# A linear-attention and MLP kernel: one layer-norm output turned by a DMA transpose instead of by TensorE, with the engines' orders around it rewritten

## The chip, the core and the metric

The kernel runs on one core of a Trainium2 chip. A core has five engines with a queue of their own each: TensorE (PE, matrix products, with a separate row PEld for the loading of its weights), VectorE (DVE), ScalarE (ACT), GpSimd (POOL) and SyncE (SP), which here only issues DMA transfers. The metric is the device time of one execution in microseconds, median over several runs.

## What is computed

Two layers, each a linear attention block and an MLP, on x of 2048 rows and 512 columns in bfloat16, 32 heads of 16, an inner width of 1792:

```python
phi = lambda t: jnp.where(t > 0, t + 1, jnp.exp(t)) + 1e-6
pq, pk = phi(q), phi(k)
kv = jnp.einsum("bhsd,bhse->bhde", pk, v)
z = jnp.einsum("bhsd->bhd", pk)
num = jnp.einsum("bhqd,bhde->bhqe", pq, kv)
den = jnp.einsum("bhqd,bhd->bhq", pq, z)[..., None] + 1e-6
...
x = x + _A_ref(_layernorm(x, axis=-1), A_wqkv, A_wo)
x = x + _B_ref(_layernorm(x, axis=-1), B_w1, B_b1, B_w2, B_b2)
x = x + _A_ref(_layernorm(x, axis=-1), A_wqkv, A_wo)
x = x + _B_ref(_layernorm(x, axis=-1), B_w1, B_b1, B_w2, B_b2)
```

`_B_ref` is gelu(y @ w1 + b1) @ w2 + b2.

## The kernel before

The 2048 rows are 16 tiles of 128 rows (0 to 15), four to a chunk (chunks 0 to 3). x stays in SBUF in float32 (`xsb`), the weights too. The kernel is a graph of operations, each with a name, an engine and the names of what it reads and writes. The order on each engine is written out by hand in the table `ORDER`, one list of names for each of PE, ACT, DVE, POOL and SP; a second table, `WAY`, says for some operations which of two ways or engines they take. The class `Scheduler` replays the lists in a model of the engines to hand out buffers and PSUM banks (the earliest free one that a class of tiles allows); `assign_waits` then sets the semaphore waits that the dependencies need. Each engine runs its list strictly in order, so an instruction that waits holds everything behind it on that engine.

How to read a name: the digit behind the letters is the layer (0 or 1), then comes the tile, or the chunk and a part of it. The stage in question is in layer two (layer digit 1), from the end of its attention to its MLP:

- `K1_t`, `Q1_c_k` are the key and query products, `expk`, `reluk`, `mink`, `phik` (and `expq` to `phiq`) the steps of phi on ACT and DVE or POOL. `G1_c_dc` are the products of a chunk's keys with its inputs, four of them; `ga1_...` and `gt1_...` add them up on DVE. `za`, `zhi`, `zlo`, `ZH1`, `Z1_3`, `zs`, `dz1`, `zb1`, `ZR1` make z and what is derived from it. `KV1`, `kvm1`, `M1` and `cpm1` fold kv and wo into one matrix.
- The denominators: chunk 0 by `D1_0_k` on PE and `ln`, `rec` on ACT; chunks 1 to 3 by `pz` (product with z), `red` (sum over a head), `den` (add 1e-6) and `rec` (reciprocal) on DVE or POOL. `pr` divides; for chunks 1 to 3 `TP1_c_k` then turns the tile by DMA.
- `WO1_t` (L1110) is the attention's output product of a tile, four matmuls into a bank of class `w` (banks 3 to 5, at most two tiles at a time in the scheduler's count). `RA1_t` (L1115) adds it to x on DVE and so frees the bank.
- The layer norm of the MLP's input: `statsB1_t` (L743) and `aggrB1_t` (L745) on DVE, `vepsB1_t` (L748) and `powB1_t` (L758, the inverse root) on POOL, then `normB1_t` on DVE (L783), or on ACT (L778) with `nmrB1_t` (L775) on POOL ahead of it.
- The normalised tile is turned into chunk buffer `yT`. There are two ways: `TB1_t`, one DMA transpose issued by SP (L793); or `PTB1_t` (L806), four TensorE transposes of 128x128 into a PSUM bank, and `tcB1_t` (L816), a copy from there on ACT. Before the change tile 0 goes the second way and tiles 1 to 15 the first.
- `W11_c_ft_h` (L1142) is one of 14 sums of the first MLP product. Chunk 0 is split in halves: h = 0 reads tiles 0 and 1 (256 columns), h = 1 tiles 2 and 3. The other chunks take all four tiles at once. `gelu1_...` (L1148) on ACT empties the bank (class `h`, banks 0 to 3).
- `W21_t_0` and `W21_t_7` (L1181) are the two halves, seven matmuls each, of the second MLP product of a tile; `RB1_t` (L1187, L1191) adds x, `OD` stores the result. `b21_t` (L1127) adds b2 to x on DVE or POOL.

ACT holds one table of functions at a time; gelu needs another than exp and ln, and each change is a table load.

The choice between the two ways of turning is made here:

```python
if eng(f"TB{L}_{st}") == "pe":
    transpose_pe(y, ykey, yT, k, f"yB{L}_{st}", prio, f"B{L}_{st}", True)
else:
    transpose(y, ykey, yT, k, f"yB{L}_{st}", prio, f"B{L}_{st}")
```

Of the kernel before, what the change touches and what calls it, by code (L numbers as in the profile page):

```python
# [1377 lines left out]
```

## Time and profile before

| what | value |
|---|---|
| median of 3 runs (lowest to highest) | 325.28 us (325.04 to 326.11) |
| the profiled execution, its own time | 324.83 us |
| its span, first to last instruction | 323.1 us |
| granted TensorE clock | 1.000 |
| busy: PE, DVE, ACT, POOL | 319.6, 215.8, 194.8, 136.4 us |
| DMA transposes of normalised tiles (L793), of attention tiles (L1078) | 58, 20 |

The profile is of one execution. Times in its rows are microseconds from the first instruction of the span. A row of the timeline has start, length, engine, line, operation, tile written <- tiles read, shapes and count; neighbours of one kind are merged, "x4" being four instructions. The bracket behind a row is idle time of the engine before it and who ended it. The ends of matmuls are modelled and overlap the next start, so TensorE is read from start to start. An ACT or DVE instruction also overlaps its neighbour by about 0.1 us at the ends. Only the engines' own work counts as busy, not the issuing of DMAs or waits.

### The profile page before, as it was taken

What the parts mean: (1) busy time and instruction counts of PE and PEld (TensorE: products, weight loads), DVE (VectorE), ACT (ScalarE), POOL (GpSimd) and SP (SyncE); (2) the same over time, 40 slices, a digit from 0 to 9 for tenths busy, and PEclk for the clock granted to TensorE, in tenths of its full rate; (3) what the DMA queues carried; (4) which work ended last, traced back from release to release, by engine and by line L of the source; (5) the groups of instructions that cost most, each with busy time, mean ns of one, the idle gap of its engine ahead of it and who ended that gap; (6) DMA issues with size and microseconds to landing.
All of it is one profiled execution on the core that took longest, in us unless ns stands there. A gap on an engine that the chain in (4) does not pass through costs nothing.

```text
span 323.1 us, 4792 instructions
## 1 busy us (share of the span) xinstructions
PE 319.6 (99%) x1725; PEld 159.0 (49%) x1725; DVE 215.8 (67%) x506; ACT 194.8 (60%) x334; POOL 136.4 (42%) x224
## 2 busy tenths in 40 slices
PE   8999999999999999999999999999999999999996
PEld 4444445675444444444444444458644444444443
DVE  5998769999985660314659999999898664000232
ACT  6999798873136139488974657879913734576000
POOL 4564376638703359000367645874902934000000
DMA  7534576213320105310003200121242242000004
GB/s 244 178 68 83 148 234 224 49 35 64 67 49 16 35 16 98 67 32 3 0 0 68 49 16 2 25 57 36 50 80 53 49 67 65 16 0 2 32 24 156
DMA packets 48116, 20.65 MB, mean 64 GB/s; under 512 B 43164, under 2 KB 46620, under 8 KB 48092
## 3 DMA queue, kind: packets, MB, share of 16 engines
q1 hardware_dynamic: 46620, 15.32, 20.7%
q0 software_dynamic: 1056, 4.72, 4.6%
q10 hardware_dynamic: 416, 0.30, 0.3%
q8 instruction: 14, 0.23, 0.3%
q14 instruction: 10, 0.08, 0.1%
...
## 4 chain that ended last, share of the span: by engine, by line
PE 92%; DVE 6%; POOL 1%; ACT 0%; issue 0%
PE ps L1142 30%; PE ps L1181 29%; PE ps L861 8%; PE ps L1110 7%; PE ps L962 4%; PE ps L879 3%; PE ps L892 3%; PE ps L994 2%; PE ps L699 1%; PE ps L1168 1%; DVE gtb L1007 1%; DVE rd L1065 1%; PE ps L943 1%; DVE xsb L1115 1%; DVE gacc L1004 1%; PE ps L1086 1%
## 5 line engine op out<-in xcount | busy, mean ns | idle before, releaser
L1148 ACT ACTIVATE gT<-ps,b1c 128x512 bf16<-128x512 f32 (+1 forms) x140 | 77.3, 601 | 64.3 <-PE ps L1142 63.4
L1142 PE MATMUL ps<-t,w 128*128 128x512 bf16 (+1 forms) x560 | 101.2, 336 | 0.0
L1181 PE MATMUL ps<-w,gT 128*128 128x512 bf16 x434 | 98.4, 379 | 0.0
L1142 PEld LDWEIGHTS ps<-t,w 128*128 128x128 bf16 x560 | 54.6, 98 | 43.7 <-ACT t L816 0.3
L1181 PEld LDWEIGHTS ps<-w,gT 128*128 128x128 bf16 x434 | 42.4, 98 | 50.0
L758 POOL TENSOR_TENSOR rstd<-veps,neghalf 128x1 f32<-128x1 f32 x64 | 39.8, 633 | 5.2 <-DVE veps L756 3.0
L1191 DVE TENSOR_TENSOR pkb<-ps,xsb 128x512 bf16<-128x512 f32 x15 | 10.2, 685 | 41.4 <-PE ps L1181 41.4
L831 ACT ACTIVATE eb<-ps 128x512 bf16<-128x512 f32 x56 | 32.4, 598 | 9.0 <-PE ps L879 3.7
L743 DVE BATCH_NORM_STATS2 stats<-xsb 128x6 f32<-128x512 f32 x48 | 32.1, 677 | 0.3
L861 PE MATMUL ps<-wqkv,t 128*128 128x512 bf16 x128 | 31.8, 379 | 0.1
L1110 PE MATMUL ps<-gtb,t 128*128 128x512 bf16 x128 | 31.2, 379 | 0.1
L842 ACT ACTIVATE rb<-ps 128x512 bf16<-128x512 f32 x38 | 22.5, 601 | 10.5 <-PE ps L861 7.2
L748 POOL TENSOR_SCALAR veps<-mv 128x1 f32<-128x1 f32 x32 | 9.1, 283 | 42.8 <-DVE mv L745 40.8
L756 POOL TENSOR_SCALAR veps<-mv 128x1 f32<-128x1 f32 x28 | 7.5, 270 | 44.4 <-DVE mv L745 42.9
L778 ACT ACTIVATE yb<-xsb,nmr,rstd 128x512 bf16<-128x512 f32 x21 | 16.7, 811 | 11.4 <-POOL nmr L775 11.4
L783 DVE TENSOR_SCALAR yb<-xsb,mv,rstd 128x512 bf16<-128x512 f32 x27 | 14.9, 559 | 11.9 <-POOL rstd L758 11.8
L1187 DVE TENSOR_TENSOR xsb<-ps,xsb 128x512 f32<-128x512 f32 x16 | 10.9, 682 | 16.7 <-PE ps L1181 16.7
L879 PE MATMUL ps<-wqkv,t 128*128 128x512 bf16 x80 | 20.4, 379 | 0.0
L861 PEld LDWEIGHTS ps<-wqkv,t 128*128 128x128 bf16 x128 | 12.2, 97 | 15.2 <-ACT t L816 0.6
L1110 PEld LDWEIGHTS ps<-gtb,t 128*128 128x128 bf16 x128 | 12.4, 98 | 14.7 <-ACT gtb L975 0.3
L844 DVE TENSOR_SCALAR eb<-eb 128x512 bf16<-128x512 bf16 x46 | 14.0, 313 | 7.1 <-ACT eb L831 6.9
L1127 POOL TENSOR_TENSOR xsb<-xsb,b2b 128x512 f32<-128x512 f32 x14 | 17.1, 1219 | 1.0 <-DVE yb L783 0.7
...
## 6 DMA issues: line engine op xcount, KB each, us to landing
...
t<-yb SPq DMA_TRANSPOSE x58, 2.5
...
t<-t SPq DMA_TRANSPOSE x20, 2.5
```

The lines of the kernel that those rows point to most:

```text
L743: G.op("dve", lambda e: e.bn_stats(stats[:, s.slot, :], src()), 602, reads=src_keys, writes=[k + "s"], tiles=[s, *src_tiles], prio=prio, n ...
L758: G.op("pool", lambda e: e.tensor_tensor(rstd[:, s.slot:s.slot + 1], veps[:, s.slot:s.slot + 1], neghalf[:], op=ALU.pow), 530, reads=[k + ...
L778: G.op("act", lambda e: e.activation(yb[:, y.slot, :], src(), ACT.Identity, bias=nmr[:, s.slot:s.slot + 1], scale=rstd[:, s.slot:s.slot + 1]),
L831: G.op("act", lambda e: e.activation(eb[:, et.slot, :], bank(bt), ACT.Exp, scale=factor()), 569 if by else 483, reads=[src_key, *more], wr ...
L842: G.op("act", lambda e: e.activation(rb[:, rt.slot, :], bank(bt), ACT.Relu, scale=factor()), 569 if by else 478, reads=[src_key, *more], w ...
L861: ins = e.matmul(bank(b), lhsT=yTa(yT)[:, dt, k * P:(k + 1) * P], rhs=wqkv[:, dt, D:2 * D], start=(dt == 0), stop=(dt == DT - 1))
L879: ins = e.matmul(bank(b), lhsT=yTa(yT)[:, dt, k * P:(k + 1) * P], rhs=wqkv[:, dt, 0:D], start=(dt == 0), stop=(dt == DT - 1))
L1110: ins = e.matmul(bank(wb), lhsT=yTa(pq)[:, kt, k * P:(k + 1) * P], rhs=gtb[:, kt, :], start=(kt == 0), stop=(kt == DT - 1))
L1127: G.op("pool" if on_pool else "dve", lambda e: e.tensor_tensor(xsb[:, st, :], xsb[:, st, :], b2b[:], op=ALU.add), 1120 if on_pool else 600 ...
L1142: ins = e.matmul(bank(b, n), lhsT=w1[:, dt, ft * P:(ft + 1) * P], rhs=yTa(yT)[:, dt, k0 * P:k1 * P], start=(dt == 0), stop=(dt == DT - 1))
L1148: G.op("act", lambda e, ft=ft, b=b, k0=k0, k1=k1, n=n: e.activation(gT[:, g.slot, ft * 512 + k0 * P:ft * 512 + k1 * P], bank(b, n), ACT.Ge ...
L1181: ins = e.matmul(bank(b), lhsT=gT[:, g.slot, ft * 512 + k * P:ft * 512 + (k + 1) * P], rhs=w2[:, ft, :], start=(ft == 0), stop=(ft == FT - 1))
```

## The change

`WAY` sends tile 0 of layer two's MLP input by DMA: `PTB1_0` and `tcB1_0` are gone, `TB1_0` on SP's queue takes their place, ahead of `TB1_1`. No other operation is added or taken away, and no way or engine of another one changes. All five lists are rewritten from the first G sums of layer two's second chunk to `W21_2_7`; behind that, and ahead of it, they are as before. In the new lists tile 0's `vepsB1` and `powB1` stand ahead of tile 1's; `WO1_14` moves into the first W1 sums; `TB1_4` to `TB1_7` go behind one another, right after `TP1_3_2`; three sums of chunk 1's W1 stand ahead of `W21_3_7`, and `W21_2_0` and `W21_2_7` come behind most of that chunk's first sums.

The diff, without the lines that only wrap differently:

```diff
-            "Q1_1_1 K1_9 G1_0_3 K1_8 W20_14_0 G1_1_1 K1_11 W20_14_7 Q1_1_2 K1_10 G1_1_3 K1_13 K1_15 K1_12 G1_1_0 "
-            "Q1_0_2 G1_1_2 Q1_0_1 K1_14 ZH1 G1_2_1 Q1_0_3 Q1_1_3 Z1_3 G1_3_1 G1_2_2 ZR1 D1_0_0 G1_2_0 Q1_3_1 G1_3_0 "
-            "D1_0_1 G1_3_2 G1_2_3 KV1_0 D1_0_2 G1_3_3 KV1_1 Q1_2_0 D1_0_3 KV1_2 Q1_3_0 KV1_3 Q1_3_2 M1_1 M1_0 M1_3 "
-            "M1_2 Q1_2_1 WO1_0_0 WO1_0_1 WO1_0_2 WO1_0_3 WO1_1_0 Q1_3_3 WO1_3_0 WO1_2_0 Q1_2_2 WO1_5_0 Q1_2_3 WO1_4_0 "
-            "PTB1_0 WO1_7_0 WO1_6_0 W11_0_13_0 W11_0_12_0 W11_0_11_0 W11_0_8_0 W11_0_9_0 W11_0_0_0 W11_0_7_0 "
-            "W11_0_5_0 W11_0_4_0 W11_0_6_0 W11_0_9_1 W11_0_10_0 W11_0_13_1 W11_0_7_1 W11_0_3_1 W11_0_1_1 W11_0_6_1 "
-            "W11_0_8_1 W11_0_11_1 W11_0_3_0 W11_0_1_0 W11_0_12_1 W11_0_2_0 W11_0_4_1 W11_0_2_1 W11_0_10_1 W11_0_0_1 "
-            "W11_0_5_1 W21_1_0 W21_0_0 W21_1_7 WO1_14_0 W21_0_7 WO1_12_0 W21_3_0 WO1_15_0 W21_3_7 W21_2_0 WO1_13_0 "
-            "W21_2_7 W11_1_1_0 W11_1_12_0 W11_1_4_0 W11_1_6_0 W11_1_2_0 WO1_8_0 W11_1_11_0 W11_1_5_0 W11_1_9_0 "
...
+            "Q1_1_1 K1_9 G1_0_3 K1_8 W20_14_0 G1_1_1 K1_11 W20_14_7 Q1_1_2 K1_10 G1_1_3 K1_13 G1_1_0 G1_1_2 K1_12 "
+            "Q1_0_1 K1_15 K1_14 G1_2_1 Q1_1_3 Q1_0_2 Q1_0_3 ZH1 Z1_3 G1_2_2 G1_3_1 ZR1 D1_0_0 G1_2_0 G1_3_2 D1_0_1 "
+            "G1_3_0 Q1_3_1 D1_0_2 G1_2_3 KV1_0 KV1_1 G1_3_3 Q1_3_0 D1_0_3 KV1_2 Q1_2_0 KV1_3 Q1_3_2 M1_0 M1_1 M1_2 "
+            "M1_3 Q1_2_1 WO1_0_0 WO1_0_1 WO1_0_2 WO1_0_3 WO1_1_0 Q1_3_3 WO1_2_0 Q1_2_3 WO1_3_0 WO1_5_0 Q1_2_2 WO1_4_0 "
+            "WO1_6_0 WO1_7_0 W11_0_4_0 W11_0_11_0 W11_0_5_0 W11_0_7_0 W11_0_13_0 W11_0_1_0 W11_0_2_0 W11_0_8_0 "
+            "W11_0_3_0 W11_0_0_0 W11_0_6_0 W11_0_12_1 W11_0_10_0 W11_0_9_1 W11_0_6_1 W11_0_4_1 W11_0_2_1 W11_0_12_0 "
+            "W11_0_13_1 W11_0_3_1 W11_0_5_1 W11_0_0_1 W11_0_7_1 W11_0_8_1 W11_0_1_1 W11_0_9_0 WO1_14_0 W11_0_11_1 "
+            "W11_0_10_1 W21_0_0 W21_1_0 W21_0_7 W21_1_7 W21_3_0 W11_1_11_0 W11_1_1_0 W11_1_2_0 W21_3_7 W11_1_6_0 "
+            "WO1_12_0 W11_1_5_0 W11_1_4_0 WO1_15_0 WO1_8_0 W11_1_10_0 W11_1_12_0 WO1_13_0 W21_2_0 W11_1_3_0 W21_2_7 "
+            "W11_1_9_0 W11_1_0_0 WO1_11_0 W11_1_13_0 WO1_10_0 W11_1_7_0 W21_6_0 WO1_9_0 W11_1_8_0 W21_5_0 W21_6_7 "
...
         "act":
...
-            "expk1_10 expq1_1_2 reluk1_10 reluk1_13 reluk1_15 expk1_13 expk1_15 expk1_12 expq1_0_1 expk1_14 expq1_0_2 "
-            "expq1_0_3 reluq1_0_2 expq1_1_3 reluq1_0_1 reluq1_0_3 cpz1 ln1_0_0 rec1_0_0 reluq1_3_1 ln1_0_1 rec1_0_1 "
-            "ln1_0_2 rec1_0_2 expq1_3_1 reluq1_1_3 ln1_0_3 rec1_0_3 cpm1_1 cpm1_2 cpm1_3 expq1_3_0 expq1_3_2 "
-            "reluq1_3_2 expq1_2_1 reluq1_3_0 expq1_3_3 reluq1_2_0 normB1_1 reluq1_2_1 expq1_2_0 reluq1_3_3 tcB1_0 "
-            "gelu1_0_13_0 gelu1_0_12_0 gelu1_0_11_0 gelu1_0_9_0 gelu1_0_8_0 gelu1_0_7_0 gelu1_0_5_0 gelu1_0_0_0 "
-            "gelu1_0_6_0 gelu1_0_4_0 gelu1_0_9_1 gelu1_0_13_1 gelu1_0_10_0 gelu1_0_3_1 gelu1_0_7_1 gelu1_0_6_1 "
-            "gelu1_0_8_1 gelu1_0_11_1 gelu1_0_1_1 gelu1_0_1_0 gelu1_0_3_0 gelu1_0_2_0 gelu1_0_12_1 gelu1_0_4_1 "
-            "expq1_2_2 expq1_2_3 gelu1_0_2_1 gelu1_0_5_1 gelu1_0_0_1 gelu1_0_10_1 normB1_6 normB1_4 normB1_7 "
-            "gelu1_1_1_0 gelu1_1_6_0 gelu1_1_2_0 gelu1_1_12_0 gelu1_1_11_0 gelu1_1_5_0 gelu1_1_4_0 gelu1_1_3_0 "
+            "expk1_10 expq1_1_2 reluk1_10 expk1_13 expk1_12 reluk1_13 reluk1_15 expk1_15 expk1_14 expq1_0_1 "
+            "reluq1_0_1 expq1_0_2 expq1_0_3 reluq1_0_3 reluq1_0_2 expq1_1_3 cpz1 ln1_0_0 rec1_0_0 ln1_0_1 reluq1_1_3 "
+            "rec1_0_1 ln1_0_2 rec1_0_2 expq1_3_1 reluq1_3_1 ln1_0_3 rec1_0_3 reluq1_3_0 reluq1_2_0 cpm1_1 cpm1_2 "
+            "cpm1_3 reluq1_3_2 expq1_3_0 expq1_3_2 reluq1_2_1 expq1_2_1 normB1_1 expq1_3_3 reluq1_3_3 expq1_2_0 "
+            "gelu1_0_4_0 gelu1_0_11_0 gelu1_0_7_0 gelu1_0_5_0 gelu1_0_13_0 gelu1_0_2_0 gelu1_0_8_0 gelu1_0_1_0 "
+            "gelu1_0_3_0 gelu1_0_0_0 gelu1_0_6_0 gelu1_0_10_0 gelu1_0_12_1 gelu1_0_6_1 gelu1_0_9_1 gelu1_0_2_1 "
+            "gelu1_0_12_0 gelu1_0_4_1 gelu1_0_13_1 gelu1_0_3_1 gelu1_0_5_1 gelu1_0_7_1 gelu1_0_8_1 gelu1_0_1_1 "
+            "normB1_7 normB1_4 gelu1_0_0_1 gelu1_0_10_1 normB1_6 gelu1_0_9_0 expq1_2_3 expq1_2_2 gelu1_0_11_1 "
+            "gelu1_1_2_0 gelu1_1_11_0 gelu1_1_1_0 gelu1_1_4_0 gelu1_1_5_0 gelu1_1_6_0 gelu1_1_12_0 gelu1_1_3_0 "
...
-            "aggrA1_14 minq1_0_0 mink1_11 phik1_11 minq1_1_2 mink1_10 normA1_14 phik1_10 phiq1_0_0 ga1_1_3 phiq1_1_2 "
-            "ga1_1_0 mink1_15 zhi1 mink1_12 zlo1 ga1_1_2 mink1_13 phik1_13 phik1_12 mink1_14 phik1_14 ga1_2_1 zsh1 "
-            "minq1_0_3 minq1_0_1 zs1_3 minq1_0_2 dz1 zb1 phiq1_0_3 phiq1_0_2 gt1_1 ga1_2_2 phiq1_0_1 red1_1_0 ga1_2_0 "
-            "gt1_0 gt1_2 red1_1_1 ga1_2_3 den1_1_0 pz1_1_2 minq1_1_3 red1_1_2 gt1_3 den1_1_1 rec1_1_0 den1_1_2 "
-            "phiq1_1_3 rec1_1_1 kvm1_1 kvm1_0 kvm1_3 kvm1_2 minq1_3_1 rec1_1_2 cpm1_0 pr1_1_1 red1_1_3 RA1_0 "
-            "statsB1_0 RA1_1 aggrB1_0 statsB1_1 den1_1_3 aggrB1_1 rec1_1_3 minq1_3_0 pr1_1_3 RA1_2 phiq1_3_0 "
-            "statsB1_2 normB1_0 aggrB1_2 RA1_5 RA1_3 statsB1_3 minq1_2_0 aggrB1_3 normB1_2 RA1_7 minq1_3_2 normB1_3 "
-            "pz1_3_1 RA1_4 red1_3_0 phiq1_2_0 phiq1_3_2 statsB1_5 statsB1_7 minq1_3_3 red1_3_1 RA1_6 aggrB1_5 "
-            "den1_3_0 phiq1_3_3 red1_3_2 statsB1_6 den1_3_2 aggrB1_6 aggrB1_7 rec1_3_2 red1_3_3 rec1_3_0 den1_3_1 "
-            "den1_3_3 rec1_3_3 statsB1_4 rec1_3_1 aggrB1_4 pr1_3_2 pr1_3_0 b21_1 pz1_2_0 pr1_3_3 minq1_2_2 minq1_2_1 "
-            "phiq1_2_2 normB1_5 RB1_1 red1_2_0 RA1_14 den1_2_0 pr1_3_1 RB1_0 statsB1_14 minq1_2_3 phiq1_2_1 phiq1_2_3 "
-            "RA1_12 pz1_2_3 pz1_2_1 RA1_15 rec1_2_0 RB1_3 pr1_2_0 red1_2_3 statsB1_15 den1_2_3 pz1_2_2 red1_2_2 "
-            "aggrB1_15 RA1_13 statsB1_12 red1_2_1 den1_2_2 aggrB1_12 rec1_2_3 rec1_2_2 statsB1_13 den1_2_1 rec1_2_1 "
-            "aggrB1_14 RA1_8 aggrB1_13 b21_7 statsB1_8 pr1_2_2 normB1_14 aggrB1_8 RA1_11 RB1_2 RA1_10 b21_6 normB1_8 "
...
+            "aggrA1_14 minq1_0_0 mink1_10 mink1_11 minq1_1_2 phik1_11 normA1_14 phik1_10 mink1_13 ga1_1_0 ga1_1_2 "
+            "phiq1_0_0 zhi1 phiq1_1_2 mink1_12 phik1_13 phik1_12 zlo1 mink1_14 mink1_15 ga1_1_3 ga1_2_1 minq1_0_1 "
+            "phik1_14 phiq1_0_1 zsh1 zs1_3 minq1_0_3 dz1 zb1 minq1_0_2 phiq1_0_3 minq1_1_3 phiq1_0_2 ga1_2_2 gt1_1 "
+            "red1_1_0 ga1_2_0 gt1_0 gt1_2 red1_1_1 ga1_2_3 pz1_1_2 den1_1_0 den1_1_1 red1_1_2 gt1_3 den1_1_2 "
+            "phiq1_1_3 minq1_3_1 rec1_1_2 kvm1_0 rec1_1_1 kvm1_1 kvm1_2 kvm1_3 cpm1_0 pr1_1_1 red1_1_3 rec1_1_0 "
+            "den1_1_3 RA1_0 rec1_1_3 statsB1_0 RA1_1 aggrB1_0 pr1_1_3 statsB1_1 aggrB1_1 minq1_3_2 minq1_3_0 normB1_0 "
+            "RA1_3 RA1_2 phiq1_3_0 RA1_5 statsB1_2 aggrB1_2 statsB1_3 aggrB1_3 RA1_6 normB1_2 minq1_3_3 normB1_3 "
+            "phiq1_3_2 b21_1 RA1_7 RA1_4 statsB1_5 aggrB1_5 statsB1_7 red1_3_2 statsB1_6 den1_3_2 aggrB1_6 aggrB1_7 "
+            "minq1_2_0 minq1_2_1 rec1_3_2 statsB1_4 pr1_3_2 aggrB1_4 phiq1_3_3 pz1_3_1 phiq1_2_0 red1_3_1 RA1_14 "
+            "den1_3_1 red1_3_3 red1_3_0 normB1_5 statsB1_14 rec1_3_1 pz1_2_0 red1_2_0 den1_3_3 phiq1_2_1 rec1_3_3 "
+            "den1_3_0 den1_2_0 pz1_2_1 rec1_3_0 pr1_3_3 pr1_3_0 minq1_2_3 red1_2_1 phiq1_2_3 aggrB1_14 minq1_2_2 "
+            "rec1_2_0 pr1_2_0 pz1_2_3 RB1_0 red1_2_3 RB1_1 pr1_3_1 RA1_12 phiq1_2_2 statsB1_12 den1_2_3 pz1_2_2 RB1_3 "
+            "den1_2_1 rec1_2_3 RA1_8 aggrB1_12 statsB1_8 red1_2_2 den1_2_2 rec1_2_1 RA1_13 statsB1_13 aggrB1_8 "
+            "normB1_14 rec1_2_2 pr1_2_2 aggrB1_13 b21_7 RA1_15 statsB1_15 aggrB1_15 RA1_11 RB1_2 RA1_10 b21_6 "
...
         "pool":
...
-            "pr1_0_1 pr1_0_2 pz1_1_3 pr1_0_3 pr1_1_0 pr1_1_2 phiq1_3_1 vepsB1_1 powB1_1 nmrB1_1 vepsB1_0 powB1_0 "
-            "vepsB1_2 powB1_2 pz1_3_0 vepsB1_3 powB1_3 pz1_3_2 pz1_3_3 b21_3 vepsB1_6 b21_2 vepsB1_7 vepsB1_5 "
-            "vepsB1_4 powB1_6 powB1_4 powB1_7 powB1_5 nmrB1_6 nmrB1_4 b21_0 nmrB1_7 vepsB1_14 pr1_2_3 pr1_2_1 "
-            "powB1_14 vepsB1_12 powB1_12 vepsB1_8 nmrB1_12 vepsB1_15 powB1_15 vepsB1_13 powB1_13 nmrB1_15 powB1_8 "
...
+            "pr1_0_1 pr1_0_2 pz1_1_3 pr1_0_3 pr1_1_2 pr1_1_0 phiq1_3_1 vepsB1_0 powB1_0 vepsB1_1 powB1_1 nmrB1_1 "
+            "pz1_3_0 vepsB1_2 powB1_2 vepsB1_3 powB1_3 pz1_3_2 b21_0 b21_3 vepsB1_7 vepsB1_6 vepsB1_4 powB1_7 powB1_4 "
+            "powB1_6 nmrB1_6 nmrB1_4 nmrB1_7 vepsB1_5 pz1_3_3 powB1_5 pr1_2_3 b21_2 vepsB1_12 pr1_2_1 vepsB1_14 "
+            "powB1_14 powB1_12 vepsB1_8 nmrB1_12 vepsB1_15 powB1_15 vepsB1_13 powB1_13 nmrB1_15 powB1_8 b21_4 "
...
         "sp":
...
-            "TA1_7 TA1_9 TA1_10 TA1_8 TA1_11 TA1_13 TA1_12 TA1_15 TA1_14 TP1_1_1 TP1_1_0 TP1_1_2 TP1_1_3 TB1_1 TB1_2 "
-            "TB1_3 TP1_3_2 TP1_3_0 TP1_3_3 TB1_6 TB1_5 TP1_3_1 TB1_4 OD1 TB1_7 OD0 TP1_2_0 TP1_2_3 TP1_2_1 TP1_2_2 "
...
+            "TA1_7 TA1_9 TA1_10 TA1_8 TA1_11 TA1_13 TA1_12 TA1_15 TA1_14 TP1_1_1 TP1_1_2 TP1_1_0 TP1_1_3 TB1_0 TB1_1 "
+            "TB1_2 TB1_3 TP1_3_2 TB1_4 TB1_5 TB1_6 TB1_7 TP1_3_0 TP1_3_3 TP1_2_0 OD0 OD1 TP1_3_1 TP1_2_1 TP1_2_3 "
+            "TP1_2_2 TB1_13 TB1_14 TB1_15 TB1_12 TB1_9 OD5 TB1_10 TB1_8 TB1_11 OD12 OD14 OD10 OD3 OD6 OD7 OD15_0 OD8 "
...
-        "TB1_0": "pe", "TB1_1": "dma", "TB1_10": "dma", "TB1_11": "dma", "TB1_12": "dma", "TB1_13": "dma",
+        "TB1_0": "dma", "TB1_1": "dma", "TB1_10": "dma", "TB1_11": "dma", "TB1_12": "dma", "TB1_13": "dma",
```

22 rows, old and new, of the table ORDER are left out of this document.

## The prediction

> **What bounds the kernel now.** I read the page's chain of waits first, then the busy time in stretches, then who made TensorE wait, and last each engine's own timeline around the removed transpose.
>
> ```profile
> PE 92%; DVE 6%; POOL 1%; ACT 0%; issue 0%
> ```
>
> TensorE owns 92% of the chain. Where, and with how little slack, is read from the stretches (start:end, length, busy time of each engine) and from the waits of its weight loader between 100 us and the end, of which the longest comes first (total, times, longest).
>
> ```profile
> 182.00:207.00 25.00, 25.00 (x151) 12.14 (x149) 24.52 (x60) 17.73 (x33) 14.69 (x14) 1.00 0.06 11
> 207.00:217.00 10.00, 9.87 (x51) 4.63 (x49) 9.46 (x24) 7.66 (x14) 7.92 (x12) 1.00 0.32 66
> 217.00:229.00 12.00, 12.00 (x112) 10.73 (x110) 11.89 (x34) 10.96 (x25) 6.56 (x9) 1.00 0.12 25
> 229.00:245.00 16.00, 16.00 (x76) 7.22 (x75) 14.71 (x32) 6.47 (x11) 5.19 (x10) 1.00 0.43 88
> ```
>
> ```profile
> PEld ps L1110 <- DVE xsb L1115: 0.3, 1, 0.3
> ```
>
> From 182 to 245 us TensorE is idle for 0.13 us in all, in 207:217, and no wait of its loader is over 0.3 us. VectorE is the runner-up: 24.52 of 25, 9.46 of 10, 11.89 of 12 us. So the end moves by TensorE instructions taken out, plus whatever TensorE newly waits for. Where TensorE passes the rewritten stretch with no wait, every later instruction simply starts earlier.
>
> TensorE around the transpose (start, length, line, count):
>
> ```profile
> 213.57 1.03 PE L1110 MATMUL ps<-gtb,t 128*128 128x512 bf16 x4
> 214.43 0.39 PE L806 MATMUL ps<-idp,yb 128*128 128x128 bf16 x4
> 214.94 1.90 PE L1110 MATMUL ps<-gtb,t 128*128 128x512 bf16 x8
> 216.68 12.39 PE L1142 MATMUL ps<-t,w 128*128 128x256 bf16 x112
> 228.91 4.70 PE L1181 MATMUL ps<-w,gT 128*128 128x512 bf16 x21
> 233.44 1.03 PE L1110 MATMUL ps<-gtb,t 128*128 128x512 bf16 x4
> ```
>
> Start to start, a four-matmul product costs 0.86 us (213.57 to 214.43), a half-width W1 sum 12.23/28 = 0.437 us, a W2 half of seven 4.53/3 = 1.51 us.
>
> **The change, part by part.** *PTB1_0 out (TensorE).* Its slot runs from 214.43 to 214.94, 0.51 us: four transposes, and behind them the 0.3 us wait of WO1_7 for a bank that RA1_5 frees. The new list has PTB1_0 nowhere and the same multiset of other products, so up to the first W1 sum TensorE is 0.51 us earlier: slot 216.17 instead of 216.68. The bank wait goes only if RA1_5 is done by then: WO1_7 now comes one product later (215.3), and RA1_5 stands three VectorE steps after normB1_0, near 214.3. If not, 0.3 us stays. Gain: between 0.2 and 0.51, I take 0.51, the slot as it stands.
>
> *tcB1_0 out (ScalarE).* It hides behind the table load before the first gelu; TensorE is the one that paces the gelus, so I price it at 0.
>
> ```profile
> 214.93 0.61 ACT L816 ACTIVATE t<-ps 128x512 bf16<-128x512 bf16 x1
> 215.55 1.28 ACT L1314 ACT_TABLE_LOAD   x1
> ```
>
> *TB1_0 in (SP's queue).* One more turn in front of TB1_1, TB1_2 and TB1_3. The next rows are TB1_1's issue and, in the DMA view of that moment, its time to landing.
>
> ```profile
> 213.61 1.19 SPq L793 DMA_TRANSPOSE t<-yb  x1
> ```
>
> ```profile
> t<-yb SPq DMA_TRANSPOSE x1, 2.4
> ```
>
> It costs 1.2 us of queue and lands 2.4 us after issue. Today tile 0 takes PTB1_0 and tcB1_0, from 214.43 to 215.54: 1.1 us. The slower way is covered only if normB1_0 comes earlier, which the new lists see to: veps and pow of tile 0 now precede tile 1's on POOL. The Trainium skill (VectorE: DVE Perf Modes, "The three transpose paths" and "Rules for kernel authors") gives 390 ns for a TensorE transpose and 1309 ns for one by DMA, and says to use TensorE where PSUM will do. That speaks against this edit; the trace agrees that the DMA is slower to land, but not that TensorE time is the cheap one here. By the rule the sum becomes the late-tile rival below; by the rows it stays.
>
> *Does the first W1 sum find tile 1?* W11_0_4_0 needs tiles 0 and 1 landed. The chain today, on VectorE, POOL and ScalarE:
>
> ```profile
> 207.72 0.69 DVE L1115 TENSOR_TENSOR xsb<-ps,xsb 128x512 f32<-128x512 f32 x1
> ...
> 210.50 0.18 DVE L745 BATCH_NORM_AGGREGATE mv<-stats 128x2 f32<-128x6 f32 x1
> 210.60 0.33 DVE L1070 RECIPROCAL rr<-rd 128x32 f32<-128x32 f32 x1
> ...
> 210.99 0.68 DVE L1074 TENSOR_TENSOR t<-t,rr 128x512 bf16<-128x512 bf16 x1
> ...
> 213.68 0.55 DVE L783 TENSOR_SCALAR yb<-xsb,mv,rstd 128x512 bf16<-128x512 f32 x1 [0.47 <-POOL rstd L758]
> 214.14 0.17 DVE L745 BATCH_NORM_AGGREGATE mv<-stats 128x2 f32<-128x6 f32 x1
> 214.23 1.26 DVE L1115 TENSOR_TENSOR xsb<-ps,xsb 128x512 f32<-128x512 f32 x2
> ```
>
> ```profile
> 209.06 1.15 POOL L848 TENSOR_TENSOR t<-eb,rb 128x512 bf16<-128x512 bf16 x1
> 210.77 0.35 POOL L748 TENSOR_SCALAR veps<-mv 128x1 f32<-128x1 f32 x1 [0.56 <-DVE mv L745]
> 211.20 0.88 POOL L758 TENSOR_TENSOR rstd<-veps,neghalf 128x1 f32<-128x1 f32 x1
> 212.18 0.55 POOL L775 TENSOR_SCALAR nmr<-mv,rstd 128x1 f32<-128x1 f32 x1
> 212.82 0.19 POOL L748 TENSOR_SCALAR veps<-mv 128x1 f32<-128x1 f32 x1
> 213.09 0.55 POOL L758 TENSOR_TENSOR rstd<-veps,neghalf 128x1 f32<-128x1 f32 x1
> ```
>
> ```profile
> 212.77 0.81 ACT L778 ACTIVATE yb<-xsb,nmr,rstd 128x512 bf16<-128x512 f32 x1 [1.45 <-POOL nmr L775]
> ```
>
> RA1_0 (207.72) is held by its product, whose slot doesn't move. Between it and aggrB1_1 the new list puts rec1_1_3 and pr1_1_3 and takes out den1_1_3: 0.25 + 0.60 less some 0.2, starts counted with the 0.08 us by which neighbours overlap. So aggrB1_1 ends at 210.68 + 0.6 = 211.3. Today TB1_1 lands 5.33 us after it (213.61 + 2.4). The same steps give 216.6. If POOL runs veps and pow as briskly as for tile 0 (0.19 and 0.55 instead of 0.35 and 0.88), and nmr loses as much, it is 0.78 us sooner, 215.8. And tile 0's two POOL steps now stand ahead; they begin near 210.3, when phiq1_3_1 is done, and may still run when aggrB1_1 ends: at worst 0.4 later, 217.0. Against the slot of 216.17 the wait lies between 0 and 0.85 us. I take 216.27 and 0.1 us, nearer the brisk end, because pr1_1_3, which today runs beside the slow pow (210.99 and 211.20), is done by then. The Trainium skill (SBUF — State Buffer, "SBUF: two separate sides") calls the port shared by VectorE and GpSimd an exclusive lock; by it, slow steps all through give 216.6 and a wait of 0.4.
>
> normB1_0 itself then runs near 211.6, so TB1_0 is off the queue at 213.4, before normB1_1 ends: it delays nothing behind it.
>
> *Tiles 2 and 3.* The first sum on them is the twelfth: 216.17 + 11 x 0.437 = 220.97. RA1_3, today the second of the two at 214.23, now follows normB1_0 at 212.1; tile 3's chain moves up by over two us, POOL then paces it. I estimate its landing at 220.4: no wait.
>
> *WO1_14 moves up*, from 233.44 to the place after 26 sums: 216.17 + 11.36 = 227.53. It needs TP1_3_2, behind pr1_3_2, today the first of these:
>
> ```profile
> 227.78 1.25 DVE L1074 TENSOR_TENSOR t<-t,rr 128x512 bf16<-128x512 bf16 x2
> ```
>
> ```profile
> L1065 DVE TENSOR_REDUCE rd<-lr 128x32 f32<-128x512 f32 x4 | 2.7, 664 | 0.0
> ...
> L1070 DVE RECIPROCAL rr<-rd 128x32 f32<-128x32 f32 x4 | 1.3, 337 | 0.0
> ...
> L1127 DVE TENSOR_TENSOR xsb<-xsb,b2b 128x512 f32<-128x512 f32 x1 | 0.7, 685 | 0.0
> ```
>
> The new list puts behind it three reduces (3 x 0.66), three reciprocals (1.0), three small adds, a z product, two phi sums and an aggregate (2.1 together): 5.1 us less twelve overlaps of 0.08 = 4.2. It adds b21_1 and a minimum ahead, 0.8. So pr1_3_2 ends near 227.78 + 0.67 - 3.4 = 225.05, or 224.4 if the 0.65 us that VectorE was idle in 207:229, the 0.47 us wait at 213.68 among them, close up; with 2.4 us the turn lands between 226.8 and 227.5. The wait is between 0 and a few tenths; I take 0.
>
> *Chunk 1's W1 sums* begin at 216.17 + 28 x 0.437 + 0.86 + 5 x 1.51 = 236.8, ahead of where W21_2_7 stands now. Their last turn, TB1_7, follows normB1_5, which stands behind RA1_14: 227.53 + 1.03 + 0.69 + two reduces and the norm = 231.0; two more turns at 1.2, then 2.4, land it at 235.8. Cover 1.0 us, price 0.
>
> Sum: -0.51 + 0.1 = -0.41 us on an execution of 324.83 (span 323.1 and 1.73 around it), 324.42. The median of the runs, 325.28, lies 0.45 above that execution; carried over, **324.9**.
>
> **The rivals.** *Tile 1 is late.* The turn chain takes the slow steps and POOL is still at tile 0: wait 0.4 to 0.85, net -0.1 to +0.35, a median near 325.4. For it: VectorE's density, and two turns now stand in one queue before the first sum, which is also what the rule on transpose paths would do here. Against: one of the two is early.
>
> *VectorE becomes the bound, and the kernel slower.* The new lists ask for RA1_14, statsB1_4 and pr1_3_2 six us sooner of an engine that is 99% busy in 217:229. VectorE steps stretch when POOL works beside them: this same b2 addition once took 1.54 us instead of 0.69.
>
> ```profile
> 258.21 1.54 DVE L1127 TENSOR_TENSOR xsb<-xsb,b2b 128x512 f32<-128x512 f32 x1
> ```
>
> b21_1 now meets pz1_3_2 on POOL: +0.85; two more hits of that size among the thirty-odd instructions up to pr1_3_2 make a slip of 2.5. It decides from the point where TP1_3_2 lands after 227.5; from the late end of that estimate nearly each us is paid at WO1_14, and RA1_14 and chunk 1's turns slip with it. Net -0.5 + 2.5 = +2.0, median 327.3; at half the slip 326.0. Against: POOL's big steps are few there.
>
> *More than the slot.* No later wait of TensorE of any size is there to be removed, so below 325.28 - 0.51 = 324.77 only scatter leads; the runs of before spread from 325.04 to 326.11.
>
> **How the numbers follow.** About 0.3%, 0.98 us, is what a measurement can tell from no change, so the full 0.51 counts as no change. Forecast 0.55 (own range 324.5 to 325.2); tile 1 late 0.2, also within; VectorE the bound 0.2, nearly all slower; scatter below 324.3, 0.05. Faster 0.07, within 0.69, slower 0.24, with some for a wait that I priced at 0. The range: 324.3, the gain with scatter, to 326.8, at three quarters of the VectorE slip.
>
> **What would show it.** Right: no L806 rows after 200 us; TensorE's first L1142 row of 256 columns in this stage at 216.2 to 216.3; L1181 starting near 229.3 after WO1_14; all products after W21_2_7 about 0.4 us earlier. Wrong: a gap before the first L1142 row (tile 1 late); a wait of the L1110 loader on a DMA near 227.5, with VectorE's aggrB1_4 past 225 (VectorE the bound); a gap at 236.8 (chunk 1's turns); or a wait for a bank, which the trace of before cannot price beyond its 0.3 us.

## The result, and the profile after

| | before | after |
|---|---|---|
| median (lowest to highest), 19 runs each | 325.24 us (325.01 to 326.26) | 324.71 us (324.33 to 325.85) |
| ratio, 95% interval | | 0.998 (0.9971 to 0.9989) |
| profiled execution, its own time | 324.83 us | 324.83 us |
| its span | 323.1 us | 323.1 us |
| busy PE, DVE, ACT, POOL | 319.6, 215.8, 194.8, 136.4 us | 319.8, 215.7, 193.7, 134.6 us |

The medians differ by 0.5 us, and yet the two profiled executions have the same span. TensorE's timeline of the kernel before at the start, at the first output product of layer two and late in its MLP:

```profile
4.73 0.40 PE L806 MATMUL ps<-idp,yb 128*128 128x128 bf16 x4
...
5.88 1.02 PE L861 MATMUL ps<-wqkv,t 128*128 128x512 bf16 x4
...
206.66 1.89 PE L1110 MATMUL ps<-gtb,t 128*128 128x512 bf16 x8
...
269.05 4.48 PE L1142 MATMUL ps<-t,w 128*128 128x512 bf16 x20
```

The same view of the changed kernel, with the rewritten stretch in the middle:

```profile
4.73 0.63 PE L806 MATMUL ps<-idp,yb 128*128 128x128 bf16 x4
...
6.43 1.13 PE L861 MATMUL ps<-wqkv,t 128*128 128x512 bf16 x4
...
207.06 1.89 PE L1110 MATMUL ps<-gtb,t 128*128 128x512 bf16 x8
...
213.97 2.75 PE L1110 MATMUL ps<-gtb,t 128*128 128x512 bf16 x12
216.65 11.53 PE L1142 MATMUL ps<-t,w 128*128 128x256 bf16 x104
228.02 1.03 PE L1110 MATMUL ps<-gtb,t 128*128 128x512 bf16 x4
228.88 1.04 PE L1142 MATMUL ps<-t,w 128*128 128x256 bf16 x8
229.75 7.72 PE L1181 MATMUL ps<-w,gT 128*128 128x512 bf16 x35
237.31 2.75 PE L1142 MATMUL ps<-t,w 128*128 128x512 bf16 x12
...
269.03 4.48 PE L1142 MATMUL ps<-t,w 128*128 128x512 bf16 x20
```

Both do their first transposes at 4.73. Then this execution of the changed kernel loses time in code that is the same in both (four transposes take 0.63 us instead of 0.40). By 11 us it is 0.41 us behind (a group of L861 starts at 11.37 instead of 10.96), and it arrives at layer two 0.40 us late (207.06 against 206.66). At 269 us it stands level (269.03 against 269.05). So the stretch between is 0.42 us shorter, and the start-up hid that in the span. Whoever compares the spans alone reads "no effect". From here on, a time of the changed kernel is compared with the prediction after adding 0.40 to the latter.

There is no L806 row in the stretch any more, and the twelve matmuls from 213.97 (three products) run without a break. How busy each engine is (start:end, length, then busy time and count of PE, PEld, DVE, ACT and POOL):

```profile
207.00:217.00 10.00, 10.00 (x50) 4.53 (x48) 9.76 (x25) 6.65 (x12) 7.88 (x13) 1.00 0.39 79
217.00:229.00 12.00, 12.00 (x109) 10.38 (x107) 9.64 (x25) 10.63 (x26) 8.38 (x15) 1.00 0.17 36
```

TensorE's idle time is gone at this resolution. VectorE, which was busy for 11.89 of 12 us in the second stretch, is busy for 9.64: it has slack now. The waits of TensorE's weight loader from 100 us to the end, the longest first:

```profile
PEld ps L1142 <- DMA t<-yb: 0.4, 1, 0.4
```

The wait for the bank that RA1_5 frees (0.3 us before) has left the list, and a wait for a turned tile stands at its head. The loader runs a little ahead of the products, so TensorE itself loses less than this: twelve matmuls of 2.59 us in all (0.216 each, start to start) from 213.97 end at 216.56, the first W1 sum starts at 216.65, so 0.09 us are lost.

### The profile page after: what moved, and what is told of

It is laid out like the page before. It is cut to its first block, busy times and chain, and to the rows that moved or that the text cites. A ratio compares the mean times of both kernels' runs of the same rounds, so it can differ in the third digit from the quotient of the medians.

```text
span 323.1 us, 4780 instructions
## 1 busy us (share of the span) xinstructions
PE 319.8 (99%) x1721; PEld 159.7 (49%) x1721; DVE 215.7 (67%) x506; ACT 193.7 (60%) x333; POOL 134.6 (42%) x224
## 4 chain that ended last, share of the span: by engine, by line
PE 99%; DVE 0%; issue 0%
PE ps L1142 30%; PE ps L1181 29%; PE ps L861 9%; PE ps L1110 9%; PE ps L879 5%; PE ps L962 4%; PE ps L994 4%; PE ps L892 3%; PE ps L699 2%; PE ps L1168 1%; PE ps L1086 1%; PE ps L943 1%; PE ps L1017 1%; PE ps L1040 1%; PE ps L806 0%; PE ps L1031 0%
## 5 line engine op out<-in xcount | busy, mean ns | idle before, releaser
L1181 PE MATMUL ps<-w,gT 128*128 128x512 bf16 x434 | 98.2, 379 | 0.0
L1181 PEld LDWEIGHTS ps<-w,gT 128*128 128x128 bf16 x434 | 42.5, 98 | 50.0
L758 POOL TENSOR_TENSOR rstd<-veps,neghalf 128x1 f32<-128x1 f32 x64 | 38.6, 614 | 5.1 <-DVE veps L756 2.9
L861 PE MATMUL ps<-wqkv,t 128*128 128x512 bf16 x128 | 31.9, 380 | 0.0
L756 POOL TENSOR_SCALAR veps<-mv 128x1 f32<-128x1 f32 x28 | 7.3, 265 | 44.6 <-DVE mv L745 43.1
L748 POOL TENSOR_SCALAR veps<-mv 128x1 f32<-128x1 f32 x32 | 7.8, 243 | 30.1 <-DVE mv L745 28.3
L861 PEld LDWEIGHTS ps<-wqkv,t 128*128 128x128 bf16 x128 | 12.4, 98 | 14.7 <-DVE eb L844 0.4
L844 DVE TENSOR_SCALAR eb<-eb 128x512 bf16<-128x512 bf16 x46 | 13.3, 299 | 7.2 <-ACT eb L831 6.9
```

The lines of the kernel that those rows point to most:

```text
L758: G.op("pool", lambda e: e.tensor_tensor(rstd[:, s.slot:s.slot + 1], veps[:, s.slot:s.slot + 1], neghalf[:], op=ALU.pow), 530, reads=[k + ...
L861: ins = e.matmul(bank(b), lhsT=yTa(yT)[:, dt, k * P:(k + 1) * P], rhs=wqkv[:, dt, D:2 * D], start=(dt == 0), stop=(dt == DT - 1))
L1181: ins = e.matmul(bank(b), lhsT=gT[:, g.slot, ft * 512 + k * P:ft * 512 + (k + 1) * P], rhs=w2[:, ft, :], start=(ft == 0), stop=(ft == FT - 1))
```

## The experiments

To compare kernels free of what each execution lost ahead of the change, one distance is read in each trace: from the start of RA1_0 on VectorE to the start of TensorE's last group (L1168, 14 matmuls). Before it is 319.68 - 207.72 = 111.96 us, after 319.66 - 208.13 = 111.53, that is 0.43 less. The ratios are each kernel's median against runs of the kernel before on the same chip.

| kernel | RA1_0 | last group | distance | against before | ratio (95% interval) |
|---|---|---|---|---|---|
| before | 207.72 | 319.68 | 111.96 | | |
| after | 208.13 | 319.66 | 111.53 | -0.43 | 0.998 (0.9971 to 0.9989) |
| old_lists_dma | 208.24 | 320.90 | 112.66 | +0.70 | 1.0021 (1.001 to 1.0032) |
| new_lists_pe | 207.69 | 319.34 | 111.65 | -0.31 | 0.999 (0.998 to 0.9999) |
| tile1_first | 207.91 | 320.75 | 112.84 | +0.88 | 1.0029 (1.0019 to 1.004) |
| tile1_chain_early | 208.34 | 320.06 | 111.72 | -0.24 | 0.9988 (0.998 to 0.9997) |
| pr_shift_small | 209.07 | 320.61 | 111.54 | -0.42 | 0.9985 (0.9975 to 0.9996) |
| pr_shift_one | 208.21 | 320.10 | 111.89 | -0.07 | 1.0001 (0.9988 to 1.0014) |
| late_pr | 208.74 | 322.21 | 113.47 | +1.51 | 1.0055 (1.004 to 1.007) |

Put as a ratio (0.1% is 0.33 us), each difference of the distance lies inside its kernel's interval, and the distance tells kernels apart that the intervals cannot. It is one execution each, however. One more kernel changes layer one, ahead of this distance, and is read in another way below. RA1_0 itself scatters from 207.69 to 209.07. The old and the new lists differ for some time ahead of RA1_0 already, but that is not where the scatter comes from: from one group of W2 matmuls ahead of the first difference (L1181, at 179.27 us before and 179.67 after) to RA1_0, all nine kernels take 28.45 or 28.46 us. So the new lists neither gain nor lose anything there, and the distance leaves out nothing of the change.

### The turn alone, and the lists alone

The change is two things at once: a turn by DMA, and new lists. `old_lists_dma` is the kernel before with the turn alone:

```diff
-"PTB1_0 WO1_7_0 WO1_6_0 W11_0_13_0 ..."
+"WO1_7_0 WO1_6_0 W11_0_13_0 ..."
...
-"reluq1_3_3 tcB1_0 gelu1_0_13_0"
+"reluq1_3_3 gelu1_0_13_0"
...
-"TP1_1_3 TB1_1 TB1_2"
+"TP1_1_3 TB1_1 TB1_0 TB1_2"
...
-"TB1_0": "pe"
+"TB1_0": "dma"
```

> Before's lists, with tile 0's turn alone moved from TensorE to SP's queue, right behind TB1_1. Theory 1 (the DMA turn pays only where the lists bring tile 0's norm forward): WO1_7 is still held by RA1_5 until 214.9, so the four transposes taken out only lengthen that wait, and the first W1 sum could start at 216.7 as before; TB1_0 leaves the queue after TB1_1, at 214.85, and lands at 217.3, so that TensorE waits 0.6 us ahead of it. Time 0.6 us above before, about 325.85, ratio 1.002. Rival (taking the transposes off TensorE is the gain, the lists are beside the point): 0.2 to 0.5 us below before, 324.75 to 325.0.

`new_lists_pe` is the changed kernel with tile 0 turned by TensorE again:

```diff
-"WO1_4_0 WO1_6_0 WO1_7_0 W11_0_4_0"
+"WO1_4_0 PTB1_0 WO1_6_0 WO1_7_0 W11_0_4_0"
...
-"expq1_2_0 gelu1_0_4_0"
+"expq1_2_0 tcB1_0 gelu1_0_4_0"
...
-"TP1_1_3 TB1_0 TB1_1"
+"TP1_1_3 TB1_1"
...
-"TB1_0": "dma"
+"TB1_0": "pe"
```

> The changed kernel's lists, with tile 0 turned by TensorE again (PTB1_0 between WO1_4 and WO1_6, tcB1_0 on ACT behind expq1_2_0, TB1_0 out of SP's list). Theory 1: the four transposes cost 0.22 us of TensorE, the wait for RA1_5's bank doesn't come back, and tile 1 has landed by then; against the changed kernel +0.22 less its wait of 0.09 = +0.13 us, about 324.85, against before -0.3, ratio 0.999. Rival (the lists carry all of the gain): as the changed kernel, 324.7. Rival (the turn carries all of it): as before, 325.2.

Measured: 325.94 us, ratio 1.0021, and 324.84 us, ratio 0.999, both as expected. TensorE's timeline of `old_lists_dma`; the bracket is idle time ahead of the row:

```profile
214.08 1.03 PE L1110 MATMUL ps<-gtb,t 128*128 128x512 bf16 x4
215.44 1.90 PE L1110 MATMUL ps<-gtb,t 128*128 128x512 bf16 x8 [0.34 <-DVE xsb L1115]
217.89 1.38 PE L1142 MATMUL ps<-t,w 128*128 128x256 bf16 x11 [0.55 <-DMA t<-yb]
```

Without the new lists the turn by DMA saves nothing and loses 0.7 us. The four transposes are out, but the next product waits for its bank until the same moment: from the end of the products before it (214.08 + 0.86) to 215.44 are 0.50 us, the slot's 0.51 of before. And behind the products TensorE waits for tile 0, which stands behind tile 1 in SP's queue. The bracket counts from the modelled end of the row before; start to start, eight matmuls from 215.44 end at 217.17, so this wait is 0.72 us, which is the whole loss of 0.70. The same view of `new_lists_pe` (its line numbers are two lower):

```profile
213.53 1.03 PE L1108 MATMUL ps<-gtb,t 128*128 128x512 bf16 x4
214.40 0.39 PE L804 MATMUL ps<-idp,yb 128*128 128x128 bf16 x4
214.62 1.89 PE L1108 MATMUL ps<-gtb,t 128*128 128x512 bf16 x8
216.35 2.89 PE L1140 MATMUL ps<-t,w 128*128 128x256 bf16 x25
```

The transposes' slot is 214.62 - 214.40 = 0.22 us where it was 0.51: the bank wait is gone though the transposes are there. So of the 0.43 us, 0.31 come from the lists (0.29 of them in this slot), which let RA1_5 finish before WO1_7, and 0.12 from the turn: 0.22 of TensorE's time less the 0.09 lost on tile 1.

### Which turn comes first

`tile1_first` is the changed kernel with two names swapped in SP's list:

```diff
-"TP1_1_3 TB1_0 TB1_1 TB1_2"
+"TP1_1_3 TB1_1 TB1_0 TB1_2"
```

> The changed kernel with TB1_0 and TB1_1 exchanged in SP's list. Theory 1 (tile 0's turn is hidden because it stands ahead, with 1.6 us to spare, while tile 1's sets the start of W1): TB1_0 leaves the queue only behind TB1_1, at 215.4 in the changed kernel's times, lands at 217.85, and the first W1 sum, whose slot is 216.56, waits 1.3 us in place of 0.09; 1.2 us above the changed kernel, about 325.9, ratio to before 1.002. Rival (a turn on the queue is hidden anyway): 324.7.

Measured: 326.23 us, ratio 1.0029 (1.0019 to 1.004), a little dearer than the 1.002 expected. SP's queue and then TensorE in `tile1_first` (lines one lower):

```profile
213.97 1.20 SPq L792 DMA_TRANSPOSE t<-yb  x1
215.21 1.26 SPq L792 DMA_TRANSPOSE t<-yb  x1
```

```profile
217.75 1.48 PE L1141 MATMUL ps<-t,w 128*128 128x256 bf16 x12 [1.24 <-DMA t<-yb]
```

Tile 1 can't be issued sooner than its norm on ScalarE allows, so putting it first gains it nothing (213.97 and the 0.22 us by which this execution is early make 214.19, against 214.18) and makes tile 0 the late one, by a whole turn: issued at 215.21, its reader starts 2.5 us later. The distance grows by 1.31 us over the changed kernel, where 1.2 was expected. That tile 0 uses the queue while tile 1's norm is still running is what makes its turn free.

### The same edit in layer one, without new lists

`layer1_tile0_dma` is the changed kernel with the turn made once more in layer one:

```diff
-"WO0_6_0 PTB0_0 WO0_7_0"
+"WO0_6_0 WO0_7_0"
...
-"expq0_2_2 tcB0_0 gelu0_0_12_0"
+"expq0_2_2 gelu0_0_12_0"
...
-"TB0_1 TB0_2"
+"TB0_1 TB0_0 TB0_2"
...
-"TB0_0": "pe"
+"TB0_0": "dma"
```

> The changed kernel with the same edit made once more in layer one and without lists searched anew there: PTB0_0 and tcB0_0 are left out, TB0_0 goes by DMA on SyncE behind TB0_1, everything else as it is. My theory: what the edit costs is decided by where its row stands in the SyncE queue. Behind TB0_1 (issued 58.46 in the changed kernel's trace) it is issued at about 59.7 and lands 2.43 us later, 62.15; its first reader stands at 61.01, and 60.79 when PTB0_0's slot of 0.23 us is gone. So a wait of 1.3 us and a slot of 0.2 less: 1.1 us more than the changed kernel, about 325.8 us, ratio to before 1.002. Rival, the turn by DMA is free wherever a queue has room, since TensorE is the bound and has four matmuls less: 324.5 us, ratio 0.998 or below.

Measured: 326.14 us, ratio 1.0013 (1.0001 to 1.0024), against the changed kernel's 0.998: +0.33%, 1.1 us, as expected. Its queue and TensorE:

```profile
59.39 1.26 SPq L793 DMA_TRANSPOSE t<-yb  x1
```

```profile
61.92 1.27 PE L1142 MATMUL ps<-t,w 128*128 128x256 bf16 x10 [1.06 <-DMA t<-yb]
```

Issued at 59.39, 2.53 us to the reader, as in layer two. Start to start, the sixteen matmuls ahead of that reader, from 57.00, end at 60.46, so it waits 1.46 us; less the 0.23 of the slot taken out, that is 1.23. From layer one's first RA0_0 to the last group the trace has 320.55 - 53.53 = 267.02 us, the changed kernel 319.66 - 53.85 = 265.81: 1.21 us more. Four transposes less on an engine that bounds the kernel are worth their 0.2 us only if the other way is not late.

### Tile 1's statistics earlier

The one wait that the change left on TensorE is 0.09 us for tile 1. `tile1_chain_early` moves one name on VectorE:

```diff
-"aggrB1_0 pr1_1_3 statsB1_1 aggrB1_1 minq1_3_2"
+"aggrB1_0 statsB1_1 aggrB1_1 pr1_1_3 minq1_3_2"
```

> The changed kernel with one row moved on VectorE: pr1_1_3 goes behind aggrB1_1 instead of ahead of statsB1_1, so that tile 1's statistics end about 0.6 us sooner (aggrB1_1 211.70 would be 211.1). My theory: the only wait that the change left on TensorE is the 0.09 us ahead of W11_0_4_0, which is tile 1's landing. With the earlier chain the SyncE queue itself is what binds: TP1_1_3 until about 212.8, TB1_0 until 214.05, then TB1_1, which took 2.43 us to land in the changed kernel's trace, so 216.5, just ahead of the slot at 216.56. The wait goes, the gain is at most 0.09 us: 324.6 us, ratio to before 0.998 (no difference that can be told from the changed kernel). Rival, the lists still hide a wait behind tile 1 worth several tenths (TP1_3_2 or reluq1_2_1 later): 324.2 us or below, ratio 0.997 or less.

Measured: 325.22 us, ratio 0.9988. The interval takes in the expected 0.998, but the trace contradicts it: the distance is 0.19 us longer, where I expected up to 0.09 less. The queue, first in the changed kernel (TP1_1_3, then TB1_1), then in this one (the same two, 0.21 us later by RA1_0):

```profile
210.93 1.27 SPq L1078 DMA_TRANSPOSE t<-t  x1
...
214.18 1.19 SPq L793 DMA_TRANSPOSE t<-yb  x1
```

```profile
211.97 1.19 SPq L1078 DMA_TRANSPOSE t<-t  x1
...
214.51 1.26 SPq L793 DMA_TRANSPOSE t<-yb  x1
```

pr1_1_3 makes the tile that TP1_1_3 turns. Moved behind, it makes TP1_1_3 0.83 us later (211.97 - 0.21 - 210.93), and through the queue TB1_1 0.12 later, although its statistics end sooner; TB1_1 then took 2.50 us to land instead of 2.43. I had seen that the queue would bind, and put TB1_1's issue at 214.05, 0.25 us too early (214.51 less 0.21 is 214.30). TensorE's loader now waits 0.6 us instead of 0.4:

```profile
PEld ps L1142 <- DMA t<-yb: 0.6, 1, 0.6
```

The rival, a hidden wait of several tenths behind tile 1, is not tested by this, since tile 1 came later and not earlier. The loader's list of the changed kernel names no such wait behind the one for tile 1; whether one would appear if tile 1 came earlier stays open.

### How far VectorE may slip

The prediction's rival on the other side was a VectorE too slow for TP1_3_2, which WO1_14 reads. Three kernels delay pr1_3_2 by steps:

```diff
-"statsB1_4 pr1_3_2 aggrB1_4 phiq1_3_3 pz1_3_1 phiq1_2_0 red1_3_1 RA1_14"
+"statsB1_4 aggrB1_4 phiq1_3_3 pr1_3_2 pz1_3_1 phiq1_2_0 red1_3_1 RA1_14"
...
+"statsB1_4 aggrB1_4 phiq1_3_3 pz1_3_1 pr1_3_2 phiq1_2_0 red1_3_1 RA1_14"
...
+"statsB1_4 aggrB1_4 phiq1_3_3 pz1_3_1 phiq1_2_0 red1_3_1 pr1_3_2 RA1_14"
```

The three lines are `pr_shift_small`, `pr_shift_one` and `late_pr`. First the largest step:

> The changed kernel with pr1_3_2 five VectorE steps later, right ahead of RA1_14 (aggrB1_4, phiq1_3_3, pz1_3_1, phiq1_2_0 and red1_3_1 go first). Theory 1 (VectorE is close to the bound at WO1_14: TP1_3_2 lands 0.76 us ahead of its slot): it lands at 229.1 instead of 227.2, the slot is 227.9, TensorE waits 1.15 us ahead of WO1_14 and the end comes 1.15 us later: about 325.85, ratio to before 1.002. Rival (VectorE's lateness is not passed on, or has more cover): within 0.2 us of the changed kernel, 324.9.

Measured: 327.28 us, ratio 1.0055 (1.004 to 1.007), about twice the cost I expected. TensorE at WO1_14, and the DMA view from 226 to 232 us, in `late_pr`:

```profile
230.79 0.81 PE L1110 MATMUL ps<-gtb,t 128*128 128x512 bf16 x3 [1.99 <-DMA t<-t]
```

```profile
q14 instruction: 1, 0.01, 0.6%
issues: line engine op xcount, KB each, median us to landing
t<-t SPq DMA_TRANSPOSE x1, 3.1
```

The transpose took 3.1 us to land, not 2.4, and a DMA packet of an instruction queue ran meanwhile (229.23 to 229.82 us, the transpose from 227.45 to 230.52). The sum closes with that: pr1_3_2 starts at 226.75, less the 0.61 by which this execution is late at RA1_0, 2.07 us later than in the changed kernel; less the cover of 0.76 us; plus 0.67 for the slow transpose (3.07 instead of the 2.40 that it took in the changed kernel): 1.98 us. The distance grew by 1.94. To see whether the cover and the price of one for one are right without the slow transpose, the two smaller shifts:

> The changed kernel with pr1_3_2 behind aggrB1_4 and phiq1_3_3 on VectorE, 0.40 us later than in the changed kernel (their steps in the row, 0.09 and 0.31 us). My theory: TP1_3_2 landed at 227.17 in the changed kernel, 0.76 us ahead of WO1_14's slot at 227.93, so a shift of 0.40 us is free: 324.7 us, ratio to before 0.998, no gap ahead of WO1_14. Rival, VectorE and TensorE are both bounds here and each tenth on the one is paid on the other: 325.1 us, ratio 0.9995.

> The changed kernel with pr1_3_2 behind aggrB1_4, phiq1_3_3 and pz1_3_1 on VectorE, 1.0 us later than in the changed kernel (steps of 0.09, 0.31 and 0.60 us). My theory: beyond the cover of 0.76 us the shift is paid one for one if the transpose takes its usual 2.4 us to land: a gap of 0.25 us ahead of WO1_14, 324.95 us, ratio to before 0.999. Rival, the transpose of TP1_3_2 is late by more when it meets an instruction-fetch packet on the DMA engines, as when pr1_3_2 stood right ahead of RA1_14 (3.07 us instead of 2.43): then a gap of 0.9 us, 325.6 us, ratio 1.001, and the trace shows a packet of an instruction queue between its issue and its landing.

Measured: 325.07 us, ratio 0.9985, and 325.5 us, ratio 1.0001. The small shift, 0.53 us in its trace (225.54 less 0.94, against 224.07), is free, as expected: its distance is within 0.01 us of the changed kernel's. In `pr_shift_one` TensorE waits, and the transpose takes its usual time (TensorE, then the DMA view from 225 to 229 us):

```profile
228.68 0.81 PE L1110 MATMUL ps<-gtb,t 128*128 128x512 bf16 x3 [0.41 <-DMA t<-t]
```

```profile
t<-t SPq DMA_TRANSPOSE x1, 2.4
```

pr1_3_2 starts at 225.28, less 0.08, 1.13 us later than in the changed kernel; beyond the cover of 0.76 are 0.37; the distance grew by 0.36. The interval of its ratio holds both 0.999 and 1.001 and decides nothing; the trace decides for one to one. The rival's condition hardly occurred: a packet of an instruction queue starts at 228.39, when the transpose is landing (228.40), and it took 2.41 us. So this run neither bears the rival out nor refutes it; `late_pr` is the case that it describes. Turned round, the two runs that pay measure the cover: 1.13 - 0.36 = 0.77 us here, 2.07 + 0.67 - 1.94 = 0.80 in `late_pr`. The wait was 0.1 us longer than I had put it because the shift was 1.13 us, not 1.0: aggrB1_4 right behind its statistics starts 0.1 us later than the spacing of the old row told.

## Why the prediction was right

324.9 us were forecast and 324.71 measured; the local sum of -0.41 us stands against -0.43 in the traces. The signs that it named came: no L806 row, the first W1 row at 216.65 (216.2 to 216.3 plus 0.40), L1181 behind WO1_14 at 229.75 (229.3 plus 0.40). Step by step, 0.40 us added to the forecast times for the start-up of this execution:

- **The slot of PTB1_0**, 0.51 us with its bank wait: right, and the wait was the larger part. The step hung on RA1_5 being done near 214.3, now 214.7, when WO1_7 comes at 215.7; its row is below. What the step had wrong is to whom the gain belongs: it gave the whole slot to taking PTB1_0 out, and its 0.29 us of bank wait go with the new lists, with PTB1_0 or without.
- **tcB1_0** at 0: right; ScalarE goes into its table load as before.
- **TB1_0** covered: right. TB1_0 is off the queue at 213.75, and TB1_1 waits for its norm until 214.15 in any case; `tile1_first` shows the price when the order is the other one.
- **Tile 1**: aggrB1_1 was to end at 211.3, tile 1 to land at 216.27, 0.1 us late. These are VectorE's and POOL's rows of the changed kernel:

```profile
211.51 0.18 DVE L745 BATCH_NORM_AGGREGATE mv<-stats 128x2 f32<-128x6 f32 x1
...
213.98 0.68 DVE L1115 TENSOR_TENSOR xsb<-ps,xsb 128x512 f32<-128x512 f32 x1
...
218.21 0.69 DVE L1127 TENSOR_TENSOR xsb<-xsb,b2b 128x512 f32<-128x512 f32 x1
...
224.07 0.67 DVE L1074 TENSOR_TENSOR t<-t,rr 128x512 bf16<-128x512 bf16 x1
...
229.08 0.69 DVE L1115 TENSOR_TENSOR xsb<-ps,xsb 128x512 f32<-128x512 f32 x1 [2.41 <-PE ps L1110]
```

```profile
211.01 0.55 POOL L758 TENSOR_TENSOR rstd<-veps,neghalf 128x1 f32<-128x1 f32 x1
211.79 0.34 POOL L748 TENSOR_SCALAR veps<-mv 128x1 f32<-128x1 f32 x1 [0.23 <-DVE mv L745]
212.21 0.73 POOL L758 TENSOR_TENSOR rstd<-veps,neghalf 128x1 f32<-128x1 f32 x1
213.04 0.26 POOL L775 TENSOR_SCALAR nmr<-mv,rstd 128x1 f32<-128x1 f32 x1
...
218.38 1.54 POOL L1062 TENSOR_TENSOR lr<-t,zrow 128x512 f32<-128x512 bf16 x1 [1.03 <-DVE t L848]
```

  aggrB1_1 ends at 211.69, 0.40 after 211.3. POOL had finished tile 0's root at 211.56 and was waiting, so the worst case (tile 0 still on POOL) didn't occur. veps and the root were nearer the slow rows (0.34 and 0.73), nmr was brisk (0.26 instead of 0.55): between the two ends, as taken. The reason given for the brisk end fails, though: pr1_1_3 was done at 210.88, and yet veps and the root, from 211.79 on, were nearer the slow rows. That the three steps together came out where they were taken is in part luck. SP issued TB1_1 at 214.18, 2.43 us before it landed, and the first sum stood at 216.65: 0.09 late.
- **Tiles 2 and 3** at 0: right; no wait of the loader names them. The cover was thinner than forecast: TB1_3 landed at 221.12, 0.34 us ahead of the twelfth sum (216.65 + 11 x 0.437 = 221.46), where 0.57 was forecast.
- **WO1_14** at 227.53: it started at 228.02, and 227.53 + 0.40 + 0.09 is 228.02. TP1_3_2's landing was put between 226.8 and 227.5 (227.2 and 227.9 here). pr1_3_2 ended at 224.74 and the turn was issued at 224.77 and landed at 227.17: the early end, in which VectorE's former idle time closes up. (The sum behind those two ends is 0.06 us off: 5.1 less twelve overlaps of 0.08 is 4.14, not 4.2.)
- **VectorE the bound**: it didn't happen. b21_1 was the hit that the rival counted on. pz1_3_2 did run on POOL beside it (218.38, the last POOL row above), and yet b21_1 took 0.69 us, not 1.54; it was POOL's step that took 1.54 us instead of 1.16. VectorE waited 2.41 us for WO1_14 ahead of RA1_14. The rival's "six us sooner" was too much as well: it holds for RA1_14, while pr1_3_2 came 4.1 us sooner (227.78 against 224.07 less 0.40). The price is real: `pr_shift_one` and `late_pr` show that beyond the cover each tenth is paid. The source of lateness did not occur, and what was left of it had a cover of 0.76 us, which was my estimate's early end.
- **Chunk 1's sums** at 236.8: they started at 237.31, and 236.8 + 0.49 is 237.29. But the cover that priced this step at 0 was wrong: 1.0 us forecast, 0.3 measured. SP's queue in the changed kernel, TP1_3_2, then TB1_4 to TB1_7:

```profile
224.77 1.19 SPq L1078 DMA_TRANSPOSE t<-t  x1
229.69 5.98 SPq L793 DMA_TRANSPOSE t<-yb  x4
```

  normB1_5 ends at 231.50, as forecast (231.0 + 0.49). From there two turns were to take 2.4 us; TB1_7 is issued at 234.47, 0.57 later than that. 0.44 of it is idle time of the queue ahead of TB1_7, whose norm was done at 228.96, and the trace names no releaser for it, so its cause stays open; the rest is a turn of 1.27 us and small gaps. It then takes 2.53 us to land instead of 2.4, at 237.00. The price stayed 0 by 0.3 us.
- **Carrying the sum to the median** was the weakest step: I added the 0.45 us by which the runs of before lay above their profiled execution. The median of the changed kernel lies 0.12 us below its own. The scatter ahead of the stretch, 1.4 us at RA1_0 over nine kernels, is larger than the effect, and one execution says little of where it lies in it. So that 324.9 came within 0.2 us of 324.71 is partly luck; -0.41 against -0.43 is the better test. The prediction also took 0.98 us as the least that a measurement can tell from no change: with 19 runs each the interval is 0.6 us wide (0.9971 to 0.9989) and lies wholly below 1.
